# Token-group buffers, held-back scores and the first M1 sums of an attention kernel with two feed-forward layers

## The chip, the cores and the metric

One NeuronCore of a Trainium2 chip runs the whole kernel. The metric is the device time of one execution in microseconds (us). TensorE (PE in the profile) does the matrix products, with its weight loads shown apart as PEld. ScalarE is ACT, VectorE is DVE, GpSimd is POOL, and SP issues the DMAs. Each engine works through a queue of its own and waits on semaphores of the others.

## The reference

Channel attention over 6016 tokens of 256 channels, then two feed-forward layers:

```python
qn = q / (np.linalg.norm(q, axis=1, keepdims=True) + 1e-06)   # norm over the tokens
kn = k / (np.linalg.norm(k, axis=1, keepdims=True) + 1e-06)
s = kn.transpose(0, 2, 1) @ qn / tau                          # 256 x 256
a = softmax(s); x = v @ a                                     # 6016 x 256
h = x @ w_in;  g = h * np.clip(h + 3.0, 0.0, 6.0) / 6.0; x = g @ w_out     # d_ff = 2048
h = x @ w_in2; r = np.maximum(h, 0.0); g = r * r; out = g @ w_out2
```

## The kernel before

The opening streams q and k. There are 47 tiles of 128 tokens, loaded in 24 groups (one tile, then 23 times two). A group sits in one of eight buffers (`wo0` to `wo7`, L327). For each tile ACT squares q and k (L297), DVE adds the squares to one of two running sums (L298, `sums[t % 2]`), and PE adds the tile to the two halves of the score matrix (`score(t, x, 0)` and `score(t, x, 1)`, L301). One `score` is two PE instructions in the profile. For the last `DEFER` = 10 tiles the second half is held back in a list `late`, so that PE has work while the norms are computed.

After the loop come, in the order in which the program writes them: the norms `nrm` (PE column sums of the squares, L386), six held scores, a chain of small DVE and ACT operations that ends in `rnorm`, its broadcast `rq_ps` (L411), the other four held scores, then `softmax` for the two halves (DVE scale and maximum, ACT exponential), the transposition of its result (`transposed`: PE, then the high part on ACT; `rest`: the low part on DVE), and M1. M1 is the softmax matrix times w_in; its rows are `mps[c4, i]`, where i is the half of the channels, and `m1_out` turns them into the weights of the first layer (a high part on ACT, L477, and a low part on DVE, L479); `m1_keep` copies them once more (ACT, L487). Between these stand `keep_busy` calls, small products whose result nobody uses (L287).

Every fp32 product of the later part is three PE matmuls on high and low parts (`passes`, L311 to L313). The weights w_in and w_out come as raw words and are converted on the chip in five steps, called here `unit[k][0]` to `unit[k][4]` (`pre[...]` and `loaded[...]` in the code): magnitude (ACT L155), sign (ACT L158 and DVE L159, L160), high (DVE L163), low (DVE L168), and the split of the result into a high part (ACT) and a low part (DVE), both L124 and L126. `loaded[0]` is the first w_out unit; `pre[1]` is the second half of the first w_in unit.

The first token block then runs in 32 steps: `product` (x times M1 weights, two k halves of three matmuls), `first` (ReLU on ACT L629, `g` on DVE L631, then its split), and `second` (two groups of three matmuls with w_out, into `acc`). `second` of a step is issued two steps later (`LAG` = 2), and the conversions of the other units stand between by a plan of places (`START`, two places to a step). The rest, from about 150 us on, runs in another scheme that the change doesn't touch.

All of it stands in `tc.manual_schedule()`: each engine's queue keeps the order of the program.

Of the kernel before, what the change touches and what calls it, by code (L numbers as in the profile page):

```python
# [16 lines left out]
P = 128  # L17
# [8 lines left out]
WMAX = max(WIDTHS)  # L26
NU = KF // 2
GROUPS = [1] + [2] * 23
DEFER = 10
LATE_AT = 6  # L30
LAG = 2
AHEAD = 3
BUSY = (6, 2, 2, 3)
M1_LEAD = 3
EARLY = 12
TAU_AT = 20
# [20 lines left out]
def attention_then_two_ffns(  # L57
# [242 lines left out]
    def score(t, x, i):  # L300
        nc.tensor.matmul(  # L301
            s_ps[i], lhsT=x[:, C + i * P:C + (i + 1) * P], rhs=x[:, :C], start=(t == 0), stop=(t == NT - 1)
        )

    def passes(ps, pairs, start=True, stop=True, more=False):


        n = len(pairs)
        for i, ((ah, al), (bh, bl)) in enumerate(pairs):
            first, last = start and i == 0, stop and i == n - 1  # L310
            nc.tensor.matmul(ps, lhsT=ah, rhs=bh, start=first, stop=False, skip_group_check=more)  # L311
            nc.tensor.matmul(ps, lhsT=al, rhs=bh, start=False, stop=False, skip_group_check=more)  # L312
            nc.tensor.matmul(ps, lhsT=ah, rhs=bl, start=False, stop=last, skip_group_check=more)  # L313

    with tc.manual_schedule():
# [3 lines left out]

        warm = small(1)  # L320
        nc.scalar.activation(warm, ones[:, 0:1], AF.Sqrt)
        keep_busy(BUSY[0], "busy0")
        late = []
        pre = []
        t = 0
        for gi, n in enumerate(GROUPS):
            src = wpool.tile([P, 1024], F32, tag=f"wo{gi % NU}", name=f"qk{gi}")[:, :2 * n * C]  # L327
# [48 lines left out]
            feed()  # L376


        for st in range(4):
            pre[1][st]()  # L380


        nrm = ps_acc.tile([P, 4], F32, tag="acc", name="nrm")
        for b in range(4):
            for m, x in enumerate(sums):
                nc.tensor.matmul(  # L386
                    nrm[:, b:b + 1], lhsT=x[:, b * P:(b + 1) * P], rhs=ones[:, 0:1], start=(m == 0), stop=(m == 1)
                )
        for a in late[:LATE_AT]:
            score(*a)  # L390
# [4 lines left out]
        pre[1][4](0)  # L395
        rec = small(4)
        nc.vector.reciprocal(rec, root)
        half = small(4)
# [5 lines left out]
        nc.vector.reciprocal(rnorm, norm)  # L404

        rq_ps = ps_acc.tile([P, C], F32, tag="acc", name="rq_ps")
        loaded[0][0]()
# [4 lines left out]
        for a in late[LATE_AT:]:  # L412
            score(*a)
        pre[1][4](1)
        loaded[0][1]()
        nc.scalar.activation(warm, ones[:, 0:1], AF.Exp)
        rq = small(C)
        nc.scalar.copy(rq, rq_ps)


        rsum = []
# [19 lines left out]
        def rest(i, e, sm, et_ps):  # L441
            nc.vector.tensor_tensor(out=et[1][:, i, :], in0=et_ps, in1=f32(et[0][:, i, :]), op=ALU.subtract)
# [10 lines left out]
        def m1_half(c4, i, j):  # L453
            if j == 0:
                mps[c4, i] = bank([P, 512], f"mp{c4}_{i}")
            passes(mps[c4, i], [(
                [t[:, i, j * P:(j + 1) * P] for t in et], [t[:, j, :] for t in wi1[c4]],
            )], j == 0, j == KC - 1)

        def m1_out(c4, k):  # L460
            mp = mps[c4, k]
            if k == 0:
                wa1[c4] = wa_tiles(c4, "wa1_")
                a21[c4] = hpool.tile(
                    [P, 2, 2, P], F32R, tag=("sa", "su", "se", "h")[c4], name=f"a21_{c4}",
                    bufs=None if c4 == 3 else 1,
                )
            m = mp.rearrange("p (u f c) -> p u f c", u=2, f=2)
            if k == 0:
                to = [  # L470
                    (m[:, :, 0, :], [t[:, :, A11, :] for t in wa1[c4]]),
                    (m[:, :, 1, :], [a21[c4][:, i, :, :] for i in range(2)]),
                ]
            else:
                to = [(m, [t[:, :, A12:S1, :] for t in wa1[c4]])]
            for x, (hi, lo) in to:
                nc.scalar.activation(hi, x, AF.Copy, scale=rsum[k])  # L477
            for x, (hi, lo) in to:
# [48 lines left out]

        x0 = {}

        def split_first(k):  # L530
            w = WIDTHS[0]
            for n in range(2):
                hi, lo = x0[k, n] = operand(0, 0, ((B11, T3), (B21, B22))[k][n])
                split(hi, lo, raw0[k][:, n, :w])

        e0 = softmax(0)
        keep_busy(BUSY[1], "busy1")
        loaded[0][2]()
        transposed(0, *e0)
        e1 = softmax(1)  # L540
        loaded[0][3]()
        loaded[0][4](0)
        rest(0, *e0)
        loaded[0][4](1)
        feed()
        row_sums(0, *e0)
        keep_busy(BUSY[2], "busy2")
        m1_half(0, 0, 0)
        transposed(1, *e1)
        rest(1, *e1)  # L550
        row_sums(1, *e1)
        m1_half(0, 0, 1)
        for k in range(KC):
            split_first(k)
        loaded[1][0]()
        m1_out(0, 0)
        for j in range(KC):
            m1_half(0, 1, j)
        m1_out(0, 1)
        m1_keep(0)  # L560
        loaded[1][1]()
        loaded[1][2]()
        keep_busy(BUSY[3], "busy3")


        x2_d = [dram.tile([P, 4, WMAX], F32, name=f"x2d{p}") for p in range(NP)]
# [36 lines left out]


        w0 = WIDTHS[0]
        steps = [(n, f) for f in range(KF) for n in range(2)]
        steps[:4] = [(0, 0), (0, 1), (1, 0), (1, 1)]
        hs = {}
        pending = []
        leftover = []  # L610

        def weight0(f, k):
            c4, u, odd = f // 4, f // 2 % 2, f % 2
            if odd and k == 0:
                return [a21[c4][:, i, u, :] for i in range(2)]
            return [t[:, u, (A12, A22)[odd] if k else A11, :] for t in wa1[c4]]

        def product(at, k):
            if at < len(steps):
                n, f = steps[at]  # L620
                if k == 0:
                    hs[at] = bank([P, WMAX], f"h0_{n}_{f}")[:, :w0]
                passes(hs[at], [(weight0(f, k), x0[k, n])], k == 0, k == KC - 1)

        def first(at_step, between):
            n, f = steps[at_step]
# [270 lines left out]
        for kk in range(KC):  # L897
            for a in range(2):
                product(a, kk)
        for a, (n, f) in enumerate(steps):  # L900
            gs = first(a, issue)
            pending.append((n, f, gs))

            part, since = divmod(a + M1_LEAD, 8)
            if 0 < part < 4 and since == 1:
                for i in range(KC):
                    m1_out(part, i)
                m1_keep(part)
            late_products = (a + 1) % 8 == 0 and a < 24
            if late_products:  # L910
                drain(LAG)
            if a:
                for kk in range(KC):
                    product(a + 1, kk)
# [60 lines left out]
```

## Time and profile before

| | |
|---|---|
| device time, median of 3 runs | 1046.11 us (1046.07 to 1046.29) |
| span of the profiled execution (first to last instruction) | 1042.9 us |
| median less span | 3.2 us |
| PE busy | 1033.4 us |
| DVE busy | 862.9 us |
| ACT busy | 665.5 us |

No time of the profiled execution other than its span is given; the 3.2 us is what lies around the span if it took as long as the runs did. A busy PE is an engine with a matmul in its pipe; ends of matmuls are modelled. Idle time of an engine counts only where the chain to the end runs through it.

### The profile page before, as it was taken

To read this page: it belongs to the slowest core of one execution; us is meant where nothing else is said; L and a number is where in the kernel's file an instruction comes from. 1 tells how busy PE (TensorE), PEld (TensorE's weight loads), DVE (VectorE), ACT (ScalarE), POOL (GpSimd) and SP (SyncE) were. 2 spreads that over 40 slices of the span, in tenths; PEclk is the share of its full clock that TensorE was granted. 3 is DMA by queue.
4 is the path that set the end of the run, shared out by engine and by line. 5 is a ranking of instruction groups with operands and counts; after the bars stand their busy time and mean duration, and the time that the engine had idled before them with its cause. 6 is when DMAs were issued, how large, how long until landed. Compare 5 with 4: busy or idle time off the path is not lost.

```text
span 1042.9 us, 12995 instructions
## 1 busy us (share of the span) xinstructions
PE 1033.4 (99%) x4630; PEld 866.2 (83%) x4630; DVE 862.9 (83%) x1461; ACT 665.5 (64%) x1200; POOL 29.6 (3%) x33
## 2 busy tenths in 40 slices
PE   9999999999999999999999999999999999999998
PEld 8877788888888888888998888888888888888997
DVE  7899968889989989988988688778688678778765
ACT  6787777787878778777876455445455455445443
POOL 0012240000000000000000000000000000000000
PEclk9999999999999999999999999999999999999999
DMA  9911204003403403222665002002001100200100
GB/s 372 344 41 41 81 1 142 1 1 116 157 0 116 157 1 116 81 72 96 229 221 187 1 1 80 1 1 75 7 1 43 39 1 1 75 1 1 41 1 36
DMA packets 25936, 77.64 MB, mean 74 GB/s; under 512 B 2832, under 2 KB 4880, under 8 KB 25872
## 3 DMA queue, kind: packets, MB, share of 16 engines
q1 hardware_dynamic: 25872, 76.82, 21.0%
q8 instruction: 36, 0.59, 0.2%
q14 instruction: 28, 0.23, 0.1%
HBM read 52.95 MB, written 23.86 MB: 74 GB/s over the span
## 4 chain that ended last, share of the span: by engine, by line
PE 91%; DVE 5%; ACT 3%; issue 1%; POOL 0%; POOLq 0%
PE acc L313 15%; PE acc L312 15%; PE acc L311 15%; PE y L312 8%; PE y L311 8%; PE y L313 7%; PE q L311 4%; PE q L313 4%; PE q L312 4%; PE s L301 4%; PE x L313 2%; PE x L311 2%; PE x L312 2%; DVE g L631 1%; DVE gs L126 1%; ACT gs L124 1%
## 5 line engine op out<-in xcount | busy, mean ns | idle before, releaser
L126 DVE TENSOR_TENSOR gs<-g,gs 128x512 fp32r<-128x512 f32 (+1 forms) x384 | 260.4, 678 | 55.6 <-ACT gs L794 46.3
L313 PE MATMUL acc<-gs,wo 128*128 128x512 f32 (+1 forms) x768 | 296.7, 386 | 1.6 <-DVE gs L126 1.4
L311 PE MATMUL acc<-gs,wo 128*128 128x512 f32 (+1 forms) x768 | 295.9, 385 | 0.4 <-ACT gs L124 0.4
L312 PE MATMUL acc<-gs,wo 128*128 128x512 f32 (+1 forms) x768 | 295.9, 385 | 0.0
L794 ACT CAST gs<-g 128x512 fp32r<-128x512 f32 (+1 forms) x352 | 208.6, 613 | 32.4 <-DVE g L785 23.3
L313 PEld LDWEIGHTS acc<-gs,wo 128*128 128x128 f32 x768 | 144.2, 188 | 31.6 <-DVE gs L126 4.8
L311 PEld LDWEIGHTS acc<-gs,wo 128*128 128x128 f32 x768 | 144.2, 188 | 27.6 <-ACT gs L124 1.0
L312 PEld LDWEIGHTS acc<-gs,wo 128*128 128x128 f32 x768 | 144.2, 188 | 26.8
L767 ACT COPY se<-y 128x512 f32<-128x512 f32 (+1 forms) x88 | 50.8, 577 | 120.6 <-PE y L313 120.3
L771 DVE TENSOR_TENSOR h<-q,se 128x512 f32<-128x512 f32 (+1 forms) x88 | 59.6, 677 | 62.8 <-ACT se L767 62.3
L767 ACT COPY su<-y 128x512 f32<-128x512 f32 (+1 forms) x88 | 50.8, 577 | 85.9 <-PE y L313 75.1
L790 DVE SCALAR_TENSOR_TENSOR g<-h 128x512 f32<-128x512 f32 (+1 forms) x144 | 96.9, 673 | 0.0
L777 ACT ACTIVATE r<-h,three 128x512 f32<-128x512 f32 (+1 forms) x120 | 85.5, 713 | 8.3 <-DVE h L771 8.0
L785 DVE SCALAR_TENSOR_TENSOR g<-r,h 128x512 f32<-128x512 f32 (+1 forms) x120 | 80.6, 672 | 3.8 <-ACT r L777 3.8
L779 ACT ACTIVATE r<-y 128x512 f32<-128x512 f32 (+1 forms) x48 | 28.3, 590 | 62.7 <-PE y L313 62.7
L771 DVE TENSOR_TENSOR h<-q,su 128x512 f32<-128x512 f32 (+1 forms) x88 | 59.5, 676 | 1.5
L771 DVE TENSOR_TENSOR h<-x,sa 128x512 f32<-128x512 f32 (+1 forms) x88 | 59.1, 672 | 0.0
L767 ACT COPY sa<-y 128x512 f32<-128x512 f32 (+1 forms) x88 | 50.7, 576 | 6.8 <-PE y L313 0.7
L790 DVE SCALAR_TENSOR_TENSOR g<-y,r 128x512 f32<-128x512 f32 (+1 forms) x48 | 32.7, 681 | 23.6 <-ACT r L779 23.0
L301 PE MATMUL s<-qk 128*128 128x256 f32 x188 | 42.2, 386 | 0.0
L301 PEld LDWEIGHTS s<-qk 128*128 128x128 f32 x188 | 36.3, 195 | 5.0
L298 DVE TENSOR_TENSOR scratch<-sq,scratch 128x512 f32<-128x512 f32 x47 | 29.3, 684 | 6.4 <-ACT sq L297 6.4
(241 smaller groups left out, 1765.7 us busy)
## 6 DMA issues: line engine op xcount, KB each, us to landing
qk<-in_qk SPq DMA_DIRECT2D x23, 512.0 KB, 7.0
wo<-in_w_out SPq DMA_DIRECT2D x16, 512.0 KB, 5.1
wi<-in_w_in SPq DMA_DIRECT2D x10, 512.0 KB, 5.2
x2d<-o SPq DMA_DIRECT2D x20, 256.0 KB, 2.4
raw<-x2d SPq DMA_DIRECT2D x10, 512.0 KB, 5.7
out<-o SPq DMA_DIRECT2D x20, 256.0 KB, 2.2
raw<-in_vt SPq DMA_DIRECT2D x8, 512.0 KB, 5.8
wo2d<-wo2s SPq DMA_DIRECT2D x8, 512.0 KB, 2.9
```

The lines of the kernel that those rows point to most:

```text
L126: eng.tensor_tensor(out=lo, in0=x, in1=f32(hi), op=ALU.subtract)
L298: nc.vector.tensor_tensor(out=sums[t % 2], in0=sq, in1=sums[t % 2], op=ALU.add)
L301: nc.tensor.matmul(s_ps[i], lhsT=x[:, C + i * P:C + (i + 1) * P], rhs=x[:, :C], start=(t == 0), stop=(t == NT - 1))
L311: nc.tensor.matmul(ps, lhsT=ah, rhs=bh, start=first, stop=False, skip_group_check=more)
L312: nc.tensor.matmul(ps, lhsT=al, rhs=bh, start=False, stop=False, skip_group_check=more)
L313: nc.tensor.matmul(ps, lhsT=ah, rhs=bl, start=False, stop=last, skip_group_check=more)
L767: nc.scalar.copy(s[tag], s["y"])
L771: nc.vector.tensor_tensor(out=s[which], in0=s[ps], in1=s[tag], op=ALU.add)
L777: nc.scalar.activation(s["r" + which], h, AF.Relu, bias=three)
L785: nc.vector.scalar_tensor_tensor(out=g, in0=s["r" + which], scalar=6.0, in1=h, op0=ALU.min, op1=ALU.mult)
L790: nc.vector.scalar_tensor_tensor(out=g, in0=h, scalar=0.0, in1=r, op0=ALU.max, op1=ALU.mult)
L794: nc.scalar.copy(gs[which][0], s["g" + which])
```

## The change

- `QK_BUFS` = 14: a token group sits in one of fourteen buffers (the eight before and `b2` to `b7`).
- `DEFER` is 19 instead of 10. The held scores are issued in parts, `LATE` = (3, 6, 5, 3) and the last two.
- The two running sums are added on DVE before the norms, and `nrm` has four products instead of eight.
- Of `pre[1]`, two steps instead of four stand ahead of the norms. The table load for the exponential (`AF.Exp`) follows the square root at once.
- The second `softmax` moves behind the first half of M1. M1's sums of c4 = 0 use an accumulator bank (`m1_first`), and their low parts come last (`passes_low_last`).
- The first four products' first k halves (`two_products(0, 0)`, `two_products(2, 0)`) stand among them; `product` then adds the second k half alone.
- All of `loaded[0]` and of `loaded[1][0..2]` and `m1_keep` stand behind `m1_out(0, 1)`.
- `keep_busy` is left only at the very start.

```diff
-DEFER = 10
-LATE_AT = 6
+DEFER = 19
+LATE = (3, 6, 5, 3)
-BUSY = (6, 2, 2, 3)
+BUSY = 6
+QK_BUFS = 14
...
+            buf = gi % QK_BUFS
+            tag = f"wo{buf}" if buf < NU else f"b{buf - NU + 2}"
+            src = wpool.tile([P, 1024], F32, tag=tag, name=f"qk{gi}")[:, :2 * n * C]
...
-        for st in range(4):
-            pre[1][st]()
+        nc.vector.tensor_tensor(out=sums[0], in0=sums[0], in1=sums[1], op=ALU.add)
+        pre[1][0]()
+        pre[1][1]()
+        late_scores(LATE[0])
         nrm = ps_acc.tile([P, 4], F32, tag="acc", name="nrm")
         for b in range(4):
...
+            nc.tensor.matmul(
+                nrm[:, b:b + 1], lhsT=sums[0][:, b * P:(b + 1) * P], rhs=ones[:, 0:1], start=True, stop=True
+            )
+        late_scores(LATE[1])
...
         e0 = softmax(0)
...
+        pre[1][4](1)
+        late_scores(LATE[2])
+        transposed(0, *e0)
+        late_scores(LATE[3])
+        split_first(0, 0)
+        rest(0, *e0)
+        row_sums(0, *e0)
+        m1_first(0)
+        late_scores(len(late) - sum(LATE))
+        split_first(0, 1)
+        e1 = []
+        m1_out(0, 0, lambda: e1.extend(softmax(1)))
+        for a in range(4):
+            begin(a)
+        two_products(0, 0)
+        transposed(1, *e1)
+        two_products(2, 0)
+        rest(1, *e1)
+        row_sums(1, *e1)
+        for n in range(2):
+            split_first(1, n)
+        m1_first(1)
+        m1_out(0, 1)
+        loaded[0][0]()
+        loaded[0][1]()
         loaded[0][2]()
+        two_products(0, 1)
         loaded[0][3]()
         loaded[0][4](0)
         loaded[0][4](1)
         feed()
+        m1_keep(0)
         loaded[1][0]()
         loaded[1][1]()
         loaded[1][2]()
...
+        def two_products(a, k):
+            both = [(hs[i], product_of(i, k)[0]) for i in (a, a + 1)]
+            for ps, ((wh, wl), (xh, xl)) in both:
+                nc.tensor.matmul(ps, lhsT=wh, rhs=xh, start=k == 0, stop=False)
+                nc.tensor.matmul(ps, lhsT=wh, rhs=xl, start=False, stop=False)
+            for ps, ((wh, wl), (xh, xl)) in both:
+                nc.tensor.matmul(ps, lhsT=wl, rhs=xh, start=False, stop=k == KC - 1)
```

## Rows read from the trace of the kernel before

**Rows 1.** The page's busy times: us, share of the span, instructions.
```profile
PE 1033.4 (99%) x4630; PEld 866.2 (83%) x4630; DVE 862.9 (83%) x1461; ACT 665.5 (64%) x1200; POOL 29.6 (3%) x33
```

**Rows 2.** Busy time by stretches: us, engines, PEclk (granted clock), DMA share, GB/s.
```profile
10.00:20.00 10.00, 10.00 (x48) 8.81 (x47) 9.97 (x18) 8.97 (x17) 0.00 (x0) 1.00 1.02 418
...
50.00:62.00 12.00, 10.83 (x48) 8.38 (x49) 10.57 (x21) 10.43 (x19) 4.22 (x4) 1.00 0.06 24
62.00:75.00 13.00, 11.90 (x49) 8.45 (x48) 12.65 (x24) 9.12 (x16) 0.00 (x0) 1.00 0.27 81
75.00:90.00 15.00, 15.00 (x68) 12.43 (x67) 13.02 (x24) 12.70 (x23) 1.31 (x1) 1.00 0.13 37
90.00:150.00 60.00, 58.45 (x249) 45.74 (x249) 50.69 (x81) 43.70 (x76) 18.81 (x15) 1.00 0.14 44
...
1038.00:1042.80 4.80, 0.78 (x4) 0.38 (x2) 0.75 (x2) 0.67 (x2) 0.00 (x0) 1.00 0.50 191
```

**Rows 3.** PE in order of time, 20 to 61 us: start, us, line, operation, idle before.
```profile
19.83 21.53 PE L301 MATMUL s<-qk 128*128 128x256 f32 x99
...
41.20 1.84 PE L386 MATMUL nrm<-both,scratch 128*128 128x1 f32 x16
...
45.58 0.61 PE L411 MATMUL rq_ps<-scratch,both 128*128 128x128 f32 x4
...
48.61 0.41 PE L438 MATMUL et_ps<-both,scratch 128*128 128x128 f32 x2 [0.25 <-issue]
...
53.44 0.83 PE L287 MATMUL busy<-both 128*128 128x128 f32 x6
...
55.97 0.39 PE L313 MATMUL h<-x,wa_0h 128*128 128x512 f32 x1
...
60.98 0.39 PE L311 MATMUL acc<-gs,wo 128*128 128x512 f32 x1
```

**Rows 4.** The squares on ACT and DVE in order of time.
```profile
23.27 2.35 ACT L297 ACTIVATE sq<-qk 128x512 f32<-128x512 f32 x4 [2.24 <-DMA qk<-in_qk]
...
33.49 7.26 DVE L298 TENSOR_TENSOR scratch<-sq,scratch 128x512 f32<-128x512 f32 x12
```

**Rows 5.** SP's own waits: us in total, times, longest.
```profile
SPq L328 <- PE s L301: 20.2, 16, 1.5
```

**Rows 6.** ACT and DVE between the norms and step 0, by time.
```profile
46.94 0.48 DVE L425 SCALAR_TENSOR_TENSOR scratch<-s,scratch 128x256 f32<-128x256 f32 x1 [0.57 <-ACT scratch L418]
...
49.24 0.68 DVE L168 CUSTOM_DVE_ANT_0 tawo<-tawo,tywo 128x1024 uint16<-128x1024 uint16 x1
...
50.01 0.62 ACT L124 CAST wo<-tawo 128x512 fp32r<-128x512 f32 x1
...
53.65 0.68 ACT L155 ACTIVATE tbwi<-raw12h 128x512 f32<-128x512 f32 x1
54.22 0.47 ACT L477 ACTIVATE wa_0h<-mp,rs 128x256 fp32r<-128x256 f32 x1
...
55.09 0.48 DVE L479 SCALAR_TENSOR_TENSOR wa_0l<-mp,rs,wa_0h 128x256 fp32r<-128x256 f32 x1 [0.29 <-ACT a L477]
...
56.00 1.35 ACT L487 ACTIVATE m<-mp,rs 128x512 f32<-128x512 f32 x2 [0.37 <-DVE a L479]
...
57.33 0.69 DVE L163 SCALAR_TENSOR_TENSOR tawi<-tbwi,tawi 128x512 int32<-128x512 int32 x1
...
57.84 0.69 ACT L629 ACTIVATE r<-h,three 128x512 f32<-128x512 f32 x1
...
58.56 0.69 DVE L631 SCALAR_TENSOR_TENSOR g<-r,h 128x512 f32<-128x512 f32 x1 [0.54 <-ACT r L629]
```

**Rows 7.** The page's DMA issues: count, KB each, us to landing.
```profile
wo<-in_w_out SPq DMA_DIRECT2D x16, 512.0 KB, 5.1
```

**Rows 8.** PE in order of time, 0 to 8 us.
```profile
1.13 2.93 PE L287 MATMUL busy<-both 128*128 128x128 f32 x12 [1.13 <-POOL both L113]
3.86 4.49 PE L301 MATMUL s<-qk 128*128 128x256 f32 x15
```

More of the change, by code (lines that the diff above doesn't have):

```diff
@@ L303, in score, with passes_low_last @@
         )
+    def passes_low_last(ps, pairs, start=True, stop=True):
+        n = len(pairs)
+        for i, ((ah, al), (bh, bl)) in enumerate(pairs):
+            nc.tensor.matmul(ps, lhsT=ah, rhs=bh, start=start and i == 0, stop=False)
+            nc.tensor.matmul(ps, lhsT=ah, rhs=bl, start=False, stop=False)
+        for i, ((ah, al), (bh, bl)) in enumerate(pairs):
+            nc.tensor.matmul(ps, lhsT=al, rhs=bh, start=False, stop=stop and i == n - 1)
     def passes(ps, pairs, start=True, stop=True, more=False):
@@ L321, in attention_then_two_ffns @@
         nc.scalar.activation(warm, ones[:, 0:1], AF.Sqrt)
-        keep_busy(BUSY[0], "busy0")
+        keep_busy(BUSY, "busy")
         late = []
@@ L326, in attention_then_two_ffns @@
         for gi, n in enumerate(GROUPS):
-            src = wpool.tile([P, 1024], F32, tag=f"wo{gi % NU}", name=f"qk{gi}")[:, :2 * n * C]
+            buf = gi % QK_BUFS
+            tag = f"wo{buf}" if buf < NU else f"b{buf - NU + 2}"
+            src = wpool.tile([P, 1024], F32, tag=tag, name=f"qk{gi}")[:, :2 * n * C]
             nc.sync.dma_start(
@@ L376, in attention_then_two_ffns, with late_scores @@
             feed()
-        for st in range(4):
-            pre[1][st]()
+        nc.vector.tensor_tensor(out=sums[0], in0=sums[0], in1=sums[1], op=ALU.add)
+        pre[1][0]()
+        pre[1][1]()
+        held_back = iter(late)
+        def late_scores(n):
+            for _ in range(n):
+                score(*next(held_back))
+        late_scores(LATE[0])
         nrm = ps_acc.tile([P, 4], F32, tag="acc", name="nrm")
         for b in range(4):
[L385 to L390, printed above, removed]
+            nc.tensor.matmul(
+                nrm[:, b:b + 1], lhsT=sums[0][:, b * P:(b + 1) * P], rhs=ones[:, 0:1], start=True, stop=True
+            )
+        late_scores(LATE[1])
         x2n = small(4)
@@ L394, in attention_then_two_ffns @@
         nc.scalar.activation(root, x2n, AF.Sqrt, scale=2.0 ** -10)
-        pre[1][4](0)
+        nc.scalar.activation(warm, ones[:, 0:1], AF.Exp)
+        pre[1][2]()
         rec = small(4)
@@ L406, in attention_then_two_ffns @@
         rq_ps = ps_acc.tile([P, C], F32, tag="acc", name="rq_ps")
-        loaded[0][0]()
         for i in range(KC):
@@ L411, in attention_then_two_ffns @@
             nc.tensor.matmul(rq_ps[:, i * P:(i + 1) * P], lhsT=ones, rhs=diag, start=True, stop=True)
[L412 to L416, printed above, removed]
         rq = small(C)
         nc.scalar.copy(rq, rq_ps)
+        pre[1][3]()
+        pre[1][4](0)
         rsum = []
@@ L455, in m1_half, with m1_pairs, m1_first, m1_out @@
                 mps[c4, i] = bank([P, 512], f"mp{c4}_{i}")
[L456 to L460, printed above, removed]
+            passes(mps[c4, i], m1_pairs(c4, i, (j,)), j == 0, j == KC - 1)
+        def m1_pairs(c4, i, js):
+            return [([t[:, i, j * P:(j + 1) * P] for t in et], [t[:, j, :] for t in wi1[c4]]) for j in js]
+        def m1_first(i):
+            mps[0, i] = ps_acc.tile([P, 512], F32, tag="acc", name=f"mp0_{i}")
+            passes_low_last(mps[0, i], m1_pairs(0, i, range(KC)))
+        def m1_out(c4, k, between=lambda: None):
             mp = mps[c4, k]
@@ L473, in m1_out @@
                 ]
+            elif c4:
+                to = [(m, [t[:, :, A12:S1, :] for t in wa1[c4]])]
             else:
-                to = [(m, [t[:, :, A12:S1, :] for t in wa1[c4]])]
+                to = [(m[:, u, :, :], [t[:, u, A12:S1, :] for t in wa1[c4]]) for u in range(2)]
             for x, (hi, lo) in to:
                 nc.scalar.activation(hi, x, AF.Copy, scale=rsum[k])
+            between()
             for x, (hi, lo) in to:
@@ L528, in attention_then_two_ffns, with split_first @@
         x0 = {}
[L530 to L534, printed above, removed]
-        e0 = softmax(0)
-        keep_busy(BUSY[1], "busy1")
+        def split_first(k, n):
+            hi, lo = x0[k, n] = operand(0, 0, ((B11, T3), (B21, B22))[k][n])
+            split(hi, lo, raw0[k][:, n, :WIDTHS[0]])
+        hs = {}
+        steps = [(n, f) for f in range(KF) for n in range(2)]
@@ new lines, in attention_then_two_ffns, with weight0, product_of, begin @@
+        steps[:4] = [(0, 0), (0, 1), (1, 0), (1, 1)]
+        def weight0(f, k):
+            c4, u, odd = f // 4, f // 2 % 2, f % 2
+            if odd and k == 0:
+                return [a21[c4][:, i, u, :] for i in range(2)]
+            return [t[:, u, (A12, A22)[odd] if k else A11, :] for t in wa1[c4]]
+        def product_of(at, k):
+            n, f = steps[at]
+            return [(weight0(f, k), x0[k, n])]
+        def begin(at):
+            n, f = steps[at]
+            hs[at] = bank([P, WMAX], f"h0_{n}_{f}")[:, :WIDTHS[0]]
@@ L538, in attention_then_two_ffns @@
+        for n in range(2):
[4 more added lines that the diff above has]
+        loaded[0][1]()
         loaded[0][2]()
-        transposed(0, *e0)
-        e1 = softmax(1)
+        two_products(0, 1)
         loaded[0][3]()
         loaded[0][4](0)
-        rest(0, *e0)
         loaded[0][4](1)
         feed()
[L546 to L554, printed above, removed]
-        loaded[1][0]()
[L556 to L560, printed above, removed]
+        m1_keep(0)
+        loaded[1][0]()
         loaded[1][1]()
         loaded[1][2]()
-        keep_busy(BUSY[3], "busy3")
         x2_d = [dram.tile([P, 4, WMAX], F32, name=f"x2d{p}") for p in range(NP)]
@@ L605, in attention_then_two_ffns, with product @@
         w0 = WIDTHS[0]
-        steps = [(n, f) for f in range(KF) for n in range(2)]
-        steps[:4] = [(0, 0), (0, 1), (1, 0), (1, 1)]
-        hs = {}
         pending = []
         leftover = []
[L612 to L618, printed above, removed]
+        def product(at):
             if at < len(steps):
[L620 to L623, printed above, removed]
+                if at > 3:
+                    begin(at)
+                passes(hs[at], [x for k in range(at < 4, KC) for x in product_of(at, k)], at > 3, True)
         def first(at_step, between):
@@ L895, in attention_then_two_ffns @@
             at(last - (NU - 2 - 2 * c4) * SLOTS + 0.1, lambda c4=c4: load_wa2(c4))
-        for kk in range(KC):
-            for a in range(2):
-                product(a, kk)
         for a, (n, f) in enumerate(steps):
@@ L912, in attention_then_two_ffns @@
             if a:
-                for kk in range(KC):
-                    product(a + 1, kk)
+                product(a + 1)
             if 0 < part < 4 and since == 0:
```

## The prediction

> **What bounds the kernel now.** I read the page's busy times first: PE is busy for 1033.4 us of a span of 1042.9 [rows 1], so all that any change to the order can win is some 9 us of waiting and whatever PE does for nobody. Then the busy times by stretches: PE is full at 10 to 20 and at 75 to 90, idle for 1.2 us at 50 to 62, 1.1 at 62 to 75, 1.55 at 90 to 150 [rows 2]. So only the passage from the scores to the steps matters. Third, PE in order of time: up to 41.2 us it runs scores back to back (99 in 21.53 us, 0.2175 each), and the norms follow without a wait [rows 3]. Last, ACT and DVE in the same passage [rows 4, 6]: the squares' adds end at 33.49 + 7.26 = 40.75, just ahead of the norms. At 62 to 75 DVE is busy for 12.65 of 13 us [rows 2]: there PE's waits are DVE's backlog.
>
> **The change part by part.** I place its instructions one behind another, engine by engine, with the durations of the rows. One matmul of the later part takes 0.228 (22 from 55.97 to 60.98, [rows 3]).
>
> *Buffers.* The loads did wait for PE's scores, 16 times, 20.2 us [rows 5], but the DMA engines were full all the same: share 1.02, 418 GB/s at 10 to 20 us [rows 2]. ACT's one long wait for a group (2.24 us, at 23.27 [rows 4]) lies in that full stretch. More buffers can't make a full queue faster, and from 33.49 DVE adds without a pause, 0.605 each. I cost the buffers at nothing: the squares still end at 40.75. The bounds are 38.5 (all of ACT's wait gone) and 41.5 (one add more).
>
> *Scores to norms.* Nine scores fewer in the loop are 18 x 0.2175 = 3.9 us, so PE leaves it at 41.2 - 3.9 = 37.3; three held ones (1.3) bring it to 38.6. The norms now need one more DVE add behind the last square (as long as the others, 0.68 with its end): 41.4. **PE waits 2.8 us there**, which it did not before. The halved norms (8 instructions of 0.115) end at 42.3; before it was 43.0.
>
> *Norms to M1's first half.* The chain from the norms to `rq_ps` took 45.58 - 43.04 = 2.5 us or less [rows 3]; six held scores (2.6) cover it, 44.9; the broadcast 0.4, 45.3. From the broadcast to the transposition it was 3.0 us [rows 3], of which 0.4 was ACT still at its table load, which now stands earlier; five held scores (2.2) cover the rest but for nothing much: 47.5. Transposition 0.4, three held (1.3) over the high part's cast, six matmuls of M1 1.4, last two held 0.9: 51.5.
>
> *Second softmax.* It needs the last held score, so it starts at 51.5 instead of 48.4. From its start to the transposition is 48.61 - 46.94 = 1.7 us [rows 3, 6], so 53.1. PE meanwhile has four products (0.9, to 52.4), then waits for M1's low parts, which stand on DVE behind the softmax's scale and maximum (0.9), at 52.9 and 53.3: done at 53.5. Transposition 0.4, six products 1.4, M1's second half 1.4: **M = 56.7** is where M1's last sum is there (before about 53.4).
>
> *From M to step 0*, the part that decides. In ACT's queue stand, ahead of step 0's ReLU: two high parts of M1, magnitude and sign of `loaded[0]`, its high split, two copies of `m1_keep`, magnitude and sign of `loaded[1]`. In the kernel before, all of `loaded[0]` had been done in the shade of the norm chain and the softmax. DVE: the first low part started only when both high parts were out (0.29 of wait for `a` [rows 6]), so M + 0.95; two low parts 0.9, sign 0.65, high 0.65, low 0.65 [rows 6]: M + 3.8. ACT has been through its own sign since M + 2.1 and waits for that; then the split 0.55, the copies 1.35, magnitude and sign 1.15: M + 6.8. ReLU 0.69, `g` 0.69, its cast 0.62 [rows 6]: **the first operand of step 0's second product is there at M + 8.9 = 65.6**. PE has to do until then only six matmuls from M + 0.5 and products 2 and 3 (six): M + 3.3. Product 4 stands behind that group in PE's queue. **PE waits 5.6 us.** Before, that group started at 60.98 without a wait [rows 3].
>
> *Removed.* Fourteen fillers of 0.14 or less (six in 0.83 [rows 3]), half of the norms (0.9) and the 1.2 us of gaps at 50 to 62: at most 4.0 us. They are in the placing above, not to be taken off again.
>
> *Behind.* DVE reaches step 0's `g` at M + 7.5 = 64.2, 5.6 later than at 58.56 [rows 6], and PE its group 4.6 later. All that comes is the same work in the same order, so the shift ends between 4.6 and 5.6; at 75 to 90 PE has no idle time to give back [rows 2]. I take 4.9, nearer the lower end, since PE was busy for 11.9 of the 13 us in which DVE held it up. Costed at nothing: the fourth w_out transfer now waits for a stage buffer until the sign step of `loaded[0]` (M + 2.5 = 59); 5.1 us to land [rows 7] makes 64, and it is due at place 13, behind six steps. SP's later issues behind it move alike. The fourth product's bank is that of the second softmax's transposition, so its matmuls may wait for DVE's `rest(1)`: 0 to 0.6, left out. Sum: 1042.9 + 4.9 = 1047.8 of span; with the 3.2 us that the median of the runs lies above the span, **1051.0**.
>
> A wait of 5.6 us is longer than any that PE has here between its first product and 1038 us. In the last 4.8 us PE is busy for 0.78 and the granted clock stays 1.00 (2.4 GHz) [rows 2]; that speaks for no loss. The Trainium skill ("TensorE: Matmul & The Clock Gate", "Why this matters for your kernels") says that gaps between bursts of matmuls can take the array back to its lower clock; the trace of before has nothing to try it on, and by that rule the last rival below would come about.
>
> **Rivals.**
> 1. *The hole is not there (faster).* If step 0's ReLU did not have to stand behind the conversions, or these ran ahead of M, PE would only do its own work: second products at M + 3.3 = 60.0, 1.0 ahead of before, and with the conversions done DVE's backlog at 62 to 75 (1.1 us) would go too: 1046.1 - 2.1 = 1044.0. For it: PE's 99%, and DVE and ACT have idle time in the new order before M. Against: in the rows each engine keeps the written order (ACT's magnitude of `loaded[1]` stands before M1's high part, as written [rows 6]). It decides where that operand comes before about M + 4.3.
> 2. *The squares end early.* If groups land earlier and ACT's 2.24 us are gone [rows 4], all behind the norms moves up by as much: 1051.0 - 2.2 = 1048.8. Against it: the full DMA engines.
> 3. *The clock falls in the hole.* PE's first 27 instructions show what a slow start costs: 12 fillers in 2.93 us against about 1.5 at the later pace, 15 score instructions in 4.49 against 3.3 [rows 3, 8], together 2.6 us: 1053.6 at most, less what DVE's backlog hides.
>
> **How the numbers follow.** The forecast (1049.8 to 1052.3 as its own range: shift 4.6 to 5.6, half a us of the placing either way, the bank's 0.6) gets 68 in 100. Rival 2 gets 10 (down to 1047.8 if PE also gains a little at the norms), rival 3 gets 9, rival 1 gets 11, of which 8 are faster by more than 0.2% and 3 within it; 2 more for a small loss or none. 0.2% (2.1 us) is about what a measurement can tell from no change. The range goes over rivals 2 and 3, 1047.8 to 1053.4, and leaves rival 1 out. Faster 0.09, same 0.05, slower 0.86.
>
> **What would show it.** In the profile after: the squares' adds end at 40 to 41 and PE waits 2 to 3 us at L386's successor for DVE's added sums; the last held score at about 51.5; PE's first `acc` matmul at 65 to 66 behind a wait of 5 to 6 us for ACT's `gs`; DVE's conversion steps of `loaded[0]` at 57 to 61. The forecast is wrong if that wait is under 3 us, if the conversions run before M1's second half, or if the adds end before 39.

## The result, and the profile after

The changed kernel takes 1053.12 us (median; 1052.77 to 1054.89) against 1046.09 (1044.48 to 1046.29): ratio 1.0074 (1.0060 to 1.0088). It is slower by 7.0 us by the medians and 7.7 by the ratio. The forecast had the sign and the place of the largest wait, but only 4.9 us of the loss. The median lies 0.3 us below the upper end of its range (1053.4). On the 1046.11 that it started from, the ratio gives 1053.9, above that range.

The page's busy times of the changed kernel, answering to [rows 1]; its span is 1051.0 us, and that execution took 1053.16:

```profile
PE 1034.2 (98%) x4608; PEld 865.9 (82%) x4608; DVE 864.0 (82%) x1463; ACT 665.2 (63%) x1201; POOL 29.0 (3%) x33
```

The engines' busy times are the same within 1.1 us; the span is 8.1 longer. So most of the loss is waiting. Stretches of the changed kernel, with the columns of [rows 2]:

```profile
50.00:62.00 12.00, 9.89 (x40) 6.59 (x38) 7.41 (x19) 4.96 (x12) 0.00 (x0) 1.00 0.09 17
62.00:66.00 4.00, 0.00 (x0) 0.00 (x0) 2.79 (x5) 3.87 (x7) 2.21 (x3) 0.79 0.54 216
66.00:70.00 4.00, 2.85 (x6) 1.97 (x7) 3.92 (x8) 2.38 (x4) 1.64 (x2) 0.50 0.00 0
70.00:75.00 5.00, 5.00 (x21) 4.01 (x21) 4.83 (x10) 4.64 (x8) 0.00 (x0) 0.88 0.37 105
75.00:90.00 15.00, 14.79 (x65) 11.90 (x64) 13.29 (x25) 11.64 (x21) 0.00 (x0) 1.00 0.13 37
125.00:128.00 3.00, 1.87 (x8) 0.89 (x6) 3.00 (x5) 1.77 (x3) 1.31 (x1) 1.00 0.01 4
128.00:133.00 5.00, 4.60 (x13) 3.64 (x14) 4.90 (x10) 3.23 (x6) 0.00 (x0) 0.66 0.00 0
```

PE does nothing at 62 to 66, and the granted clock behind it is 0.50 (1.2 GHz). It is 0.66 once more at 128 to 133, behind 1.1 us of waiting at 125 to 128. PE in order of time, answering to [rows 3]:

```profile
41.42 1.05 PE L404 MATMUL nrm<-both,scratch 128*128 128x1 f32 x8 [1.99 <-DVE scratch L391]
...
45.00 0.61 PE L428 MATMUL rq_ps<-scratch,both 128*128 128x128 f32 x4
...
47.73 0.41 PE L452 MATMUL et_ps<-both,scratch 128*128 128x128 f32 x2
...
55.23 0.50 PE L577 MATMUL h<-x,a 128*128 128x512 f32 x1 [0.45 <-DVE rs L460]
...
57.18 0.62 PE L313 MATMUL mp<-wi1h,etl 128*128 128x512 f32 x2
...
67.16 0.80 PE L321 MATMUL acc<-gs,wo 128*128 128x512 f32 x1 [5.75 <-ACT gs L125]
67.75 0.63 PE L322 MATMUL acc<-gs,wo 128*128 128x512 f32 x1
...
72.00 0.39 PE L321 MATMUL acc<-gs,wo 128*128 128x512 f32 x1
...
83.43 0.39 PE L321 MATMUL acc<-gs,wo 128*128 128x512 f32 x1
...
129.66 0.63 PE L321 MATMUL h<-x,a 128*128 128x512 f32 x1
130.08 0.63 PE L322 MATMUL h<-x,a 128*128 128x512 f32 x1
...
151.48 0.39 PE L321 MATMUL acc<-gs,wo 128*128 128x512 f32 x1
```

Two lines of the kernel before that these are set against:

```profile
76.90 0.39 PE L311 MATMUL acc<-gs,wo 128*128 128x512 f32 x1
...
143.30 0.39 PE L311 MATMUL acc<-gs,wo 128*128 128x512 f32 x1
```

M1's last sum is there at 57.8, and step 0's second product at 67.16 instead of 60.98, behind 5.75 us of waiting. What ACT does in that time, answering to [rows 6]:

```profile
57.84 0.84 ACT L498 ACTIVATE wa_0h<-mp,rs 128x256 fp32r<-128x256 f32 x2 [2.08 <-PE mp L313]
58.57 0.67 ACT L156 ACTIVATE tbwo<-wo 128x512 f32<-128x512 f32 x1
59.12 0.68 ACT L159 ACTIVATE tywo<-wo 128x512 int32<-128x512 uint32 x1
61.84 0.62 ACT L125 CAST wo<-tawo 128x512 fp32r<-128x512 f32 x1 [2.04 <-DVE tawo L169]
62.37 1.26 ACT L509 ACTIVATE m<-mp,rs 128x512 f32<-128x512 f32 x2
63.52 0.66 ACT L156 ACTIVATE tbwi<-raw12h 128x512 f32<-128x512 f32 x1
64.07 0.67 ACT L159 ACTIVATE tywi<-raw12h 128x512 int32<-128x512 uint32 x1
64.62 0.69 ACT L673 ACTIVATE r<-h,three 128x512 f32<-128x512 f32 x1
```

DVE by time at the end of that stretch, in the changed kernel:

```profile
64.76 1.10 DVE L164 SCALAR_TENSOR_TENSOR tawi<-tbwi,tawi 128x512 int32<-128x512 int32 x1
65.78 0.67 DVE L675 SCALAR_TENSOR_TENSOR g<-r,h 128x512 f32<-128x512 f32 x1
```

ACT goes through the conversions and copies one by one before the ReLU, as written; 2.04 us of it is waiting for DVE, which has the same units in its queue.

The loss in steps, by the starts of PE's `acc` matmuls in the two profiled executions: the first +6.18 (60.98 to 67.16), the seventh +7.7 (64.26 to 72.00), the 25th +6.5 (76.90 to 83.43), the 151st +8.2 (143.30 to 151.48), the span +8.1. Two parts then: 6.5 us are there by 83 us, and 1.6 come at 129 to 133, where matmuls start 0.43 us apart instead of 0.23.

### The profile page after: what moved, and what is told of

Read it like the earlier page. It is cut to its first block, busy times and chain, and to the rows that moved or that the text cites. A ratio compares the mean times of both kernels' runs of the same rounds, so it can differ in the third digit from the quotient of the medians.

```text
span 1051.0 us, 12946 instructions
## 1 busy us (share of the span) xinstructions
PE 1034.2 (98%) x4608; PEld 865.9 (82%) x4608; DVE 864.0 (82%) x1463; ACT 665.2 (63%) x1201; POOL 29.0 (3%) x33
## 4 chain that ended last, share of the span: by engine, by line
PE 89%; DVE 5%; ACT 3%; DMA 2%; issue 1%; SPq 0%; DVEq 0%; ACTq 0%
PE acc L323 16%; PE acc L322 15%; PE acc L321 15%; PE y L322 7%; PE y L323 7%; PE y L321 7%; PE q L322 4%; PE q L321 4%; PE q L323 4%; DMA qk<-in_qk 2%; PE x L323 2%; PE x L321 2%; PE x L322 2%; DVE g L675 1%; DVE gs L127 1%
## 5 line engine op out<-in xcount | busy, mean ns | idle before, releaser
L821 ACT ACTIVATE r<-y,three 128x512 f32<-128x512 f32 (+1 forms) x40 | 26.9, 673 | 12.0 <-PE y L323 11.3
```

What stands on the lines that cost most here:

```text
L821: nc.scalar.activation(s["r" + which], h, AF.Relu, bias=three)
```

## The experiments

"Before" is the kernel before, run beside each experiment on the same chip; its medians lay between 1045.25 and 1046.47. So kernels of different groups are compared by their ratios to it, which stand behind each time with a 95% interval. "Useless products" are products whose result nothing reads. M is, as in the forecast, the time at which M1's last sum is there.

**Buffers alone.** Before, with the fourteen buffers.

```diff
-            src = wpool.tile([P, 1024], F32, tag=f"wo{gi % NU}", name=f"qk{gi}")[:, :2 * n * C]
+            buf = gi % 14
+            tag = f"wo{buf}" if buf < NU else f"b{buf - NU + 2}"
+            src = wpool.tile([P, 1024], F32, tag=tag, name=f"qk{gi}")[:, :2 * n * C]
```

> The kernel before with fourteen instead of eight buffers for token groups and nothing else changed. Forecast: the adds of the squares end at 40 to 41 us as before, and the time is within 0.6 us of 1046.1. If more buffers bring the groups earlier: the adds end 1 to 2 us earlier and the time falls by 0.5 to 2 us. If loads that run ahead crowd each other: over 1047.

1045.48 us, ratio 0.9998 (0.9989 to 1.0007). SP's 20.2 us of waiting for PE's scores [rows 5] are gone, the adds end at 40.82: no gain. The forecast's *Buffers* stands, and rival 2 falls.

**The clock in the hole.** The changed kernel with 24 useless products in PE's 5.75 us, to keep the clock up.

```diff
+            if a == 2:
+                fill = ps_acc.tile([P, P], F32, tag="acc", name="fill")
+                for _ in range(24):
+                    nc.tensor.matmul(fill, lhsT=ones, rhs=ones, start=True, stop=True)
             drain(LAG)
```

> The changed kernel with 24 useless 128x128 products (two PE instructions each) between product 3 and the first second product, so PE has something to run in the hole of 5.75 us. If the hole sets the start and the fallen clock adds to it: the first acc matmul still stands at 67 us, the granted clock stays 1.00 at 62 to 75, the matmuls behind it come at 0.228 instead of 0.43 us, and the time falls by 1.0 to 1.9 us, to 1051.2 to 1052.1. If DVE's backlog hides the slower matmuls anyway: the clock stays up and the time stays within 0.4 us of 1053.1. If PE's own wait isn't what counts: no change either.

1052.64 us, 1.0067 (1.0052 to 1.0082). PE by time in this kernel:

```profile
61.40 5.52 PE L962 MATMUL fill<-both 128*128 128x128 f32 x48
...
67.34 0.50 PE L321 MATMUL acc<-gs,wo 128*128 128x512 f32 x1 [0.43 <-ACT gs L125]
...
83.61 0.39 PE L321 MATMUL acc<-gs,wo 128*128 128x512 f32 x1
...
150.02 0.39 PE L321 MATMUL acc<-gs,wo 128*128 128x512 f32 x1
```

Its stretch behind the hole, and the one in which the clock fell again in the changed kernel, with the columns of [rows 2]:

```profile
66.00:70.00 4.00, 3.21 (x18) 2.32 (x17) 3.92 (x8) 2.48 (x5) 1.83 (x2) 1.00 0.00 0
...
128.00:133.00 5.00, 4.99 (x21) 3.96 (x22) 4.90 (x9) 3.59 (x7) 0.00 (x0) 1.00 0.00 0
```

The clock stays at 1.00, and the 25th `acc` matmul still starts at 83.61 (83.43 without the products): PE's slow matmuls at 66 to 71 were hidden by DVE, busy for 3.92 of 4 us in both kernels. The median is 0.5 us under the changed kernel's, which fits neither forecast clearly; the profile speaks for the second, that DVE's backlog hides the slow matmuls. Its 151st `acc` matmul is 1.5 us earlier than the changed kernel's (150.02 to 151.48), all of it after 83 us: the granted clock at 128 to 133 is 1.00 here. The two executions with a mean clock of 0.999 and 1.000 took 1051.40 (the profiled one) and 1052.38, the two at 0.997 1053.05 and 1052.89.

**One unit ahead of M1.** The changed kernel with `loaded[0]` put back between the norm chain and M1.

```diff
+        loaded[0][0]()
+        loaded[0][1]()
         rq = small(C)
...
         pre[1][4](1)
+        loaded[0][2]()
+        loaded[0][3]()
...
         split_first(0, 0)
+        loaded[0][4](0)
...
         split_first(0, 1)
+        loaded[0][4](1)
+        feed()
...
-        loaded[0][0]()
...
-        feed()
         m1_keep(0)
```

> The changed kernel with the conversion of the first w_out unit moved back ahead of the last M1 sum (its steps into the idle times of ACT and DVE between the norms and M1's first half); m1_keep and the second w_in unit stay where the change put them. If the queue of ACT and DVE behind the last M1 sum makes the hole: PE's wait for step 0 falls from 5.75 to about 3 us, the clock does not fall there, and the time falls by 4 to 5 us, to 1048 to 1049. If the loss is made earlier, by the nine more held scores and PE's wait at the norms: the time stays above 1051.5.

1050.49 us, 1.0045 (1.0030 to 1.0060); PE's wait for step 0 is 2.5 us instead of 5.75. Less was won (0.0029, 3.0 us, by the ratios) than the wait lost, and less than the forecast's 4 to 5 us. The granted clock still falls behind the wait, to 0.75 at 66 to 70 us.

**All units ahead.** Besides, `loaded[1][0..2]` stand among M1's products, and `m1_keep` behind step 0.

```diff
         m1_out(0, 0, lambda: e1.extend(softmax(1)))
+        loaded[1][0]()
...
             split_first(1, n)
+        loaded[1][1]()
+        loaded[1][2]()
...
-        m1_keep(0)
-        loaded[1][0]()
-        loaded[1][1]()
-        loaded[1][2]()
...
+            if a == 0:
+                m1_keep(0)
```

> As unit0_early, and also the first three steps of the next w_in unit moved ahead of the last M1 sum, and m1_keep moved behind step 0. If the queue makes the hole: PE's wait for step 0 is under 1.2 us, no fall of the clock near it, and the time is 1045.5 to 1047, level with the kernel before. If the loss is made earlier: above 1050.

1050.02 us, 1.0043 (1.0028 to 1.0057). PE by time:

```profile
41.36 1.05 PE L404 MATMUL nrm<-both,scratch 128*128 128x1 f32 x8 [2.34 <-DVE scratch L391]
42.27 4.52 PE L302 MATMUL s<-qk 128*128 128x256 f32 x12
46.63 0.61 PE L428 MATMUL rq_ps<-scratch,both 128*128 128x128 f32 x4
...
63.64 0.50 PE L321 MATMUL acc<-gs,wo 128*128 128x512 f32 x1 [0.59 <-ACT gs L125]
```

The hole is shut (0.59 us), and the kernel is still 4.5 us slower than before, so most of this is made earlier than the hole. Behind the wait at the norms the six held scores took 4.52 us; in the changed kernel's own profiled execution it was 2.84. The granted clock at 40 to 45 is 0.74 here. A fall of the clock behind PE's wait at the norms is a cost that the forecast didn't have.

**The queue alone.** The kernel before, with `loaded[0]` and `loaded[1][0]` moved behind M1's last sum as in the change, and nothing else; `m1_keep`, `loaded[1][1]` and `loaded[1][2]` stood there already and now stand behind `loaded[0]`.

```diff
-        loaded[0][0]()
...
-        loaded[0][1]()
...
-        loaded[0][2]()
...
-        loaded[0][3]()
-        loaded[0][4](0)
...
-        loaded[0][4](1)
-        feed()
...
-        loaded[1][0]()
...
         m1_out(0, 1)
+        for st in range(4):
+            loaded[0][st]()
+        loaded[0][4](0)
+        loaded[0][4](1)
+        feed()
         m1_keep(0)
+        loaded[1][0]()
         loaded[1][1]()
```

> The kernel before with only this of the change: all five steps of the first w_out unit's conversion, and the first three of the next w_in unit's, stand behind the last M1 sum as in the changed kernel; eight buffers, ten held scores, fillers and products as before. If the queue behind the last M1 sum is the cause: ACT's first ReLU comes 3 to 4 us later than before, PE waits 1.5 to 3 us ahead of its first acc matmul, and the time is 2.5 to 4 us above the kernel before, some 1048 to 1049.5. If the loss needs the held scores: within 1 us of before.

1047.90 us, 1.0024 (1.0013 to 1.0034). Step 0's ReLU starts at 60.99, 3.15 later than in [rows 6], and PE waits 2.30 us at 60.03 for ACT's copies. The move costs by itself: 2.5 us by the ratio, the lower end of its forecast. PE's first `acc` matmul is 3.5 us later than before, against 6.2 in the change. PE still has twelve product matmuls to run between that wait and that matmul (64.48); that this makes the move cheaper is argued, not shown.

**Held scores alone.** Before, with the buffers and `DEFER` = 19, dealt 3, 6 and 10.

```diff
-DEFER = 10
+DEFER = 19
...
+        for a in late[:3]:
+            score(*a)
         nrm = ps_acc.tile([P, 4], F32, tag="acc", name="nrm")
...
-        for a in late[:LATE_AT]:
+        for a in late[3:3 + LATE_AT]:
...
-        for a in late[LATE_AT:]:
+        for a in late[3 + LATE_AT:]:
```

> The kernel before with fourteen buffers and nineteen held scores (three ahead of the norms, six and ten behind), conversions, fillers and M1 as before. If PE's wait at the norms is a loss by itself: PE waits 2.5 us there, the last M1 sum comes 3 to 4 us later than before, and the time is 2 to 4 us above before. If the held scores only take the place of waits that PE had anyway: within 1 us.

1049.03 us, 1.0033 (1.0020 to 1.0045). PE by time in this kernel:

```profile
40.42 2.70 PE L390 MATMUL nrm<-both,scratch 128*128 128x1 f32 x16 [1.03 <-DVE scratch L298]
42.98 5.43 PE L301 MATMUL s<-qk 128*128 128x256 f32 x12
```

Its stretch from the norms on, with the columns of [rows 2]:

```profile
40.00:45.00 5.00, 4.58 (x21) 4.22 (x22) 3.75 (x13) 1.64 (x4) 0.00 (x0) 0.64 1.02 419
```

After a wait of only 1.03 us (forecast 2.5) the clock is 0.64 for the stretch, and M is at 58.43, 4.8 later than before. The clock isn't all of it: the one execution with a mean clock of 1.000 took 1047.36, still 1.8 above before, and the ten scores behind the broadcast take PE 4.48 us (48.69 to 53.17) where the four of before took 1.89.

**Eight held scores ahead of the norms**, to fill the wait there.

```diff
-LATE = (3, 6, 5, 3)
+LATE = (8, 6, 5, 0)
```

> The changed kernel with the held scores dealt out as (8, 6, 5, 0) instead of (3, 6, 5, 3) and two, so that PE has work until the norms. PE's wait at the norms of 2.0 us goes. If PE's own work sets the last M1 sum, that sum comes 1.5 to 2 us earlier than at 57.8 and the time falls by as much; if the chain of softmax and M1 sets it, it comes under 0.7 us earlier and the time stays within 0.8 us of the changed kernel's.

1052.44 us, 1.0065 (1.0052 to 1.0079). The wait at the norms is 0.4 us, but M is at 57.60, 0.2 earlier. By the forecast's test the chain of softmax and M1 on ACT and DVE sets it, not PE's own work.

**The change's norm chain alone**: sums added on DVE, four products, the early table load.

```diff
+        nc.vector.tensor_tensor(out=sums[0], in0=sums[0], in1=sums[1], op=ALU.add)
...
-            for m, x in enumerate(sums):
...
+        nc.scalar.activation(warm, ones[:, 0:1], AF.Exp)
+        pre[1][2]()
```

> The kernel before with only the change's norm chain: one add of the two running sums, four norm products, two steps of the w_in unit behind instead of ahead of the norms, the exponential's table right behind the square root. The norms start at 41.4 instead of 41.2 and end 0.6 earlier, the broadcast comes 0.5 us earlier, and so does the first M1 sum; the time falls by 0.3 to 1.0 us against before. If DVE's later work takes it back: no difference.

1044.95 us, 0.9996 (0.9987 to 1.0005). `rq_ps` is 0.5 us earlier, M 0.2; at the end nothing that can be told from no change.

**Ten held scores in the changed kernel.**

```diff
-DEFER = 19
-LATE = (3, 6, 5, 3)
+DEFER = 10
+LATE = (0, 6, 4, 0)
```

> The changed kernel with ten held scores instead of nineteen, dealt out as (0, 6, 4, 0); all else as in the changed kernel. If the order on ACT and DVE sets everything behind the norms: the last M1 sum comes 0.5 to 1.2 us earlier than 57.8, because the second softmax starts a little earlier, PE's wait for step 0 stays near 5.7 us, and the time falls by only 0.4 to 1.4 us, to 1051.7 to 1052.7. If PE's work behind the norms sets it: nine scores of 0.43 us less give 3 to 4 us, 1049 to 1050.

1052.17 us, 1.0058 (1.0045 to 1.0072). M is at 57.01, the wait for step 0 still 5.8, as the first of the two forecasts has it. With as many held scores as before, the change still loses 6.1 of the 7.7 us.

**The second softmax early**: `loaded[0]` ahead, ten held scores, and `softmax(1)` behind the first transposition as before.

```diff
         transposed(0, *e0)
+        e1 = softmax(1)
...
-        e1 = []
-        m1_out(0, 0, lambda: e1.extend(softmax(1)))
+        m1_out(0, 0)
```

> As unit0_early, with ten held scores dealt out as (0, 6, 4, 0) and the second softmax right behind the first one's transposition, as in the kernel before. If the late second softmax, which needs the last held score, is what makes the last M1 sum late: that sum comes at 55 to 56 instead of 57.8, and the time falls against unit0_early by 1.5 to 2.5 us, to 1048 to 1049. If M1's own order (first products ahead of the second transposition) makes it late: it stays at 57 or later and the time within 0.8 us of unit0_early's 1050.5.

1051.89 us, 1.0059 (1.0043 to 1.0074), slower than both forecasts. DVE, with the softmax and the conversions ahead, writes M1's first low operand at 51.81 only, PE waits for it, and M is at 60.43 (L462, which the profile names, is the next instruction in DVE's queue):

```profile
52.28 0.73 PE L313 MATMUL mp<-wi1h,etl 128*128 128x512 f32 x2 [2.23 <-DVE rs L462]
```

**The early conversion.** Before, with the conversion that stands among the squares set two groups earlier.

```diff
-EARLY_AT = {15: (0, 1), 16: (2,), 18: (3, 4)}
+EARLY_AT = {13: (0, 1, 2), 14: (3,), 15: (4,)}
```

> The kernel before with only the first w_in unit's conversion moved two groups earlier, into the stretch in which DVE waits 2.07 us for a group. The adds of the squares end at 39.3 to 39.6 instead of 40.75, but PE leaves its scores at 41.2 as before, so the norms don't start earlier: time within 0.5 us of before. If DVE's backlog at 62 to 75 were what counts, the 1.3 us that DVE is ahead would show: 1 us faster or more.

1045.72 us, 0.9999 (0.9990 to 1.0008). The squares' adds end at 38.64, earlier than forecast, but PE leaves its scores no earlier and the time is the same.

**Early conversion, norm chain, buffers and 13 held scores**, on the kernel before, with its order of M1 and of the conversions, without the fillers `busy1`.

```diff
-DEFER = 10
+DEFER = 13
-EARLY_AT = {15: (0, 1), 16: (2,), 18: (3, 4)}
+EARLY_AT = {13: (0, 1, 2), 14: (3,), 15: (4,)}
...
-        keep_busy(BUSY[1], "busy1")
```

> The kernel before with the change's norm chain, fourteen buffers, the first w_in unit's conversion two groups earlier, thirteen held scores instead of ten (six behind the norms, seven behind the broadcast) and the fillers of the first softmax left out. Here the squares end early enough for the held scores to be worth something: the norms start at 40.0 to 40.3 instead of 41.2, the last M1 sum comes at 52.0 to 52.8 instead of 53.6, and the time is 0.8 to 1.8 us under before. If DVE's backlog takes it back: within 0.5 us of before.

1044.52 us, 0.9983 (0.9975 to 0.9992): faster than both the kernel before and the changed one. DVE by time in it:

```profile
22.05 0.42 DVE L159 TENSOR_SCALAR tawi<-raw11h 128x512 int32<-128x512 int32 x1
...
27.87 10.90 DVE L298 TENSOR_TENSOR scratch<-sq,scratch 128x512 f32<-128x512 f32 x18
38.80 0.69 DVE L381 TENSOR_TENSOR scratch<-scratch 128x512 f32<-128x512 f32 x1
```

PE by time in it:

```profile
40.15 0.95 PE L388 MATMUL nrm<-both,scratch 128*128 128x1 f32 x8
...
43.63 0.61 PE L413 MATMUL rq_ps<-scratch,both 128*128 128x128 f32 x4
```

The adds end 2.0 us earlier because DVE converts while it would wait for a group, and PE, which leaves its scores early, meets the norms without a wait; M is at 52.52, 1.1 earlier than before. PE's first `acc` matmul is nevertheless 1.2 later (62.16), since the clock falls to 0.86 at 50 to 62 us, and the 25th is 0.6 earlier (76.27 to 76.90), as is the 151st (142.67 to 143.30). The ratio's interval is 0.8 to 2.6 us. No run had this kernel with ten held scores, so what the three more of them bring is not shown.

**What is left of the order.** Two edits of the kernel with all units ahead. The first has ten held scores, so that PE has no long wait at the norms:

```diff
-DEFER = 19
-LATE = (3, 6, 5, 3)
+DEFER = 10
+LATE = (0, 6, 4, 0)
```

> As units_early (both units ahead of the last M1 sum, m1_keep behind step 0), with ten held scores dealt out as (0, 6, 4, 0): no wait at the norms. What is left of the change is the order of M1 and of the first products, and the late second softmax. If the nine more held scores and the fall of the clock at the norms make the 4.5 us that units_early is still above before: the time is 1045.5 to 1046.8 (norms_only's 1045 or little more). If the order of M1 makes them: the last M1 sum still comes 3 us later than in norms_only, PE's first acc matmul at 61 to 62, and the time is 1047.5 to 1049.5.

The second has nine useless products ahead of the norms:

```diff
         late_scores(LATE[0])
+        fill = bank([P, P], "fill", "y")
+        for _ in range(9):
+            nc.tensor.matmul(fill, lhsT=ones, rhs=ones, start=True, stop=True)
```

> As units_early, with nine useless 128x128 products ahead of the norms, in PE's wait of 2.3 us there. If that wait lets the clock fall and the chain behind it pays for the slow matmuls: granted clock 1.00 at 40 to 50, the broadcast at 45.0 instead of 46.6, and the median 1.0 to 2.0 us under units_early's 1050.0. If the slow matmuls are hidden behind DVE and ACT: within 0.6 us of it.

1048.14 us (1.0028; 1.0016 to 1.0039) and 1048.32 us (1.0028; 1.0018 to 1.0039): the first where the forecast for the order of M1 has it, the second where the forecast for the clock has it. With the nine products the stretch at the norms is at full clock (0.74 without them), in the columns of [rows 2]:

```profile
40.00:45.00 5.00, 5.00 (x36) 4.55 (x35) 4.25 (x14) 2.38 (x5) 0.00 (x0) 1.00 1.02 419
```

Its 25th `acc` matmul:

```profile
80.54 0.39 PE L321 MATMUL acc<-gs,wo 128*128 128x512 f32 x1
```

Ten held scores, or nineteen with the wait at the norms filled, end at the same ratio: in this order of the later part, held scores cost nothing that can be told and bring nothing. What is left, 1.0028, is the new order of M1, of the first products and of the second softmax, with the fillers left out and the units in their new places; no run parts these. In the profile with ten held scores M is at 58.00, 4.6 later than the norm chain alone has it (53.44); the first `acc` matmul is 1.4 later (62.19 to 60.78), the 25th 3.6 (80.29 to 76.72).

## Why the prediction came out as it did

*Held.* The adds ended at 40.64 (forecast 40.75), `rq_ps` came at 45.00 (44.9), the transposition at 47.73 (47.5). PE's wait at the norms was 1.99 us (2.8; PE left its scores 0.8 later than forecast), the hole 5.75 us (5.6), for the operand that was named and behind the queue that was named: all units put ahead shut it. The placing engine by engine carried this.

*The step that failed* is the last term, *Behind*: a shift of 4.9 us, kept to the end because "all that comes is the same work in the same order". The span moved by 8.1. By the profile the 3.2 us between are:
- 1.1 in the second softmax and M1, where the shift starts: M came at 57.8 instead of 56.7. Of it 0.45 is the wait for `rest(1)`, which has the bank of the fourth product (PE at 55.23; the profile names L460, the next instruction of DVE, from which that product takes nothing). The forecast named this wait and left it out.
- 0.4 from M to step 0's operand, 9.3 instead of 8.9: DVE's L164 took 1.10 us, not 0.69. GpSimd was busy then (2.21 us at 62 to 66). In five more kernels here this step took 1.09 or 1.10 with GpSimd busy. But in the kernel before it took 0.69 ([rows 6], at 57.33) with GpSimd busy as well, so the cause is not shown.
- 1.6 at 129 to 133, from the clock, where the work was the same but its pace was not. The four executions of the changed kernel had a mean clock of 0.993 to 0.995, those of before, beside the experiments, 0.998 to 1.000.

With the first two, PE's group was 6.2 late and DVE's `g` 7.2 (58.56 to 65.78) instead of 4.6 and 5.6. The shift of 6.5 at the 25th `acc` matmul lies between, and it is still 6.5 at the 97th (113.73 to 120.24). So the rule that the shift ends between PE's lateness and DVE's held up to there, with starting values 1.5 us too low, and it failed at the fall of the clock.

Of the time, 1.0 us went back: the 3.2 us around the span were too much. The profiled execution after has 2.2, and the executions of before have about 2.1 wherever both numbers are known. So 1051.0 was put 1 us too high by its start and 3.2 too low by its shift: that it is only 2.1 us from the median is luck. Nor does the forecast's own range follow from its terms: a shift of 4.6 to 5.6, half a us either way and 0.6 for the bank make 1050.2 to 1052.8, not 1049.8 to 1052.3.

*The price of the parts*, from the ratios (0.001 is 1.05 us). All units ahead took 1.0074 to 1.0043, so the queue behind M1 costs 3.2 us (2.5 alone in the kernel before). Useless products at the norms took 1.0043 to 1.0028, 1.6 us. The order that is left costs 2.9. The intervals are 0.0010 to 0.0015 to either side, so each of the first two is good to about 2 us only, and the second is not clear of zero. Nor is that second price a part of what the changed kernel's profile shows: there the clock stayed at 1.00 behind the wait at the norms (the six scores took 2.84 us, against 4.52 with all units ahead), and what the clock cost came at 129. By the profiles, with full clock at the norms, the 25th `acc` matmul is 6.5 us late in the changed kernel and 3.6 late with all units ahead and the nine products (80.54 to 76.90). That gives 2.9 for the queue and 3.6 for the order, and 1.6 for the clock at 129. The buffers and the norm chain cost nothing that can be told.

*Rivals.* Rival 1 was not seen: the queue kept its order and the wait was there. Its price was wrong too: all units ahead make the case that it puts at 1044.0, and that kernel takes 1050.02. Rival 2 fell with the buffers alone; the place where the squares can be had earlier is DVE's queue, not the loads. Rival 3 came about in the hole, and DVE's backlog hid its price, as the rival allowed. Two other falls of the clock were on no list: at 129 to 133 in the changed kernel, and behind the wait at the norms in others. The granted clock at 66 to 70 us, behind the hole, is 0.50. The Trainium skill ("TensorE: Matmul & The Clock Gate", "Why this matters for your kernels") says that idle gaps between bursts of matmuls take the array back to its lower clock; the trace agrees there (5.75 us of idle PE, then 0.50).

*Open.* How the 2.9 us of the order divide between the late second softmax, the shared bank and the low parts put last; the one run meant to separate the softmax put a new wait in DVE's queue instead. And why the clock falls at the norms or at 129 us in some profiles and not in others: with useless products in the hole PE waits for 1.2 us at 125 to 128 as well, and the clock stays at 1.00. That the products done ahead of M1's end bring little because ACT and DVE, not PE, set the pace at 41 to 75 us fits all runs (eight scores moved ahead of the norms: M 0.2 earlier), but was not shown by itself.

## What to carry to other kernels

Where PE is busy for 99% and still waits, find the engine that sets the pace of that passage and move work out of its queue; work taken off PE, or done by PE ahead of time, brought next to nothing here (0.2 us of M for eight scores). Matrix work that is held back only makes a wait where what it is to cover does not start earlier too: here 2 us when the squares ended as before. Thirteen held scores were part of the fastest kernel, in which DVE's queue was cleared first. Before conversions are moved behind a result, count every instruction between that result and the next one that the bottleneck needs, on each engine, as if they ran one after the other.

## What the runs showed of the hardware

- The granted clock fell after short waits in otherwise full stretches, but not each time. At 40 to 45 us it was 0.64 after 1.03 us of idle PE at the norms (held scores alone) and 0.74 after 2.34 (all units ahead). It was 1.00 after 1.99 (the changed kernel), 1.93 (useless products in the hole) and 1.86 (one unit ahead). In all five PE had run scores back to back until the wait. In the fastest kernel it was 0.56 at 56 to 58 us, after three waits of 0.38 to 0.48.
- With nine useless products in that wait it stayed at 1.00. Since it also did in three profiles without them, this one profile doesn't show that the products kept it; the mean clocks point that way (0.996 to 0.998 without, 0.998 to 1.000 with). Behind the hole the evidence is stronger: 0.50 at 66 to 70 us in three profiles with a hole of 5.75 to 5.77 us (the changed kernel, eight held scores ahead of the norms, ten held scores), 1.00 in the one with products in it.
- A slow clock need not cost. The matmuls at 0.50 in the hole's wake (66 to 71 us) were free: DVE was busy for 3.92 of 4 us there, and the 25th `acc` matmul was no earlier at full clock (83.61 to 83.43). Those of 129.2 to 132.6, 0.43 apart instead of 0.23, cost 1.6 us.
- More buffers took away 20.2 us of waiting for loads, and the adds ended at 40.82 instead of 40.75: the waiting had cost nothing.
